# A gated linear recurrence on one core: one decay-weighted pair product per chunk and head, from running sums of log decays, in place of seven doubling levels

## The chip, the core and the metric

The kernel runs on one NeuronCore of a Trainium2 chip. Its engines work side by side and each takes its own instructions in order: TensorE (PE for matrix products, PEld for the loads of their stationary operand), VectorE (DVE), ScalarE (ACT), GpSimd (POOL), and SyncE (SP), which here starts the transfers between memory and the chip. The metric is device time in microseconds (us) of the whole program. Before the change it is 1557.96 us, the median of three runs from 1555.92 to 1559.28.

## The reference

Two blocks follow each other, in float32. The first is a recurrence over 768 steps for 4 batches x 8 heads, with a 48x48 state per head and a complex gate per step and row. The second is h * erf(softplus(h)) between two matrix products, over 3072 tokens.

```python
batch, n_heads, seq, head_dim = (4, 8, 768, 48)
# a_re = rand * 0.1 + 0.85, a_im = randn * 0.1, q, k, v = randn * 0.1
mag = np.sqrt(a_re * a_re + a_im * a_im)
scale = np.minimum(mag, 0.999) / (mag + 1e-06)
a_re_n, a_im_n = (a_re * scale, a_im * scale)
for t in range(S):
    new_re = ar * S_re - ai * S_im
    new_im = ar * S_im + ai * S_re
    kv = np.einsum('bhd,bhe->bhde', k[:, :, t], v[:, :, t])
    S_re, S_im = (new_re + kv, new_im)
    y[:, :, t] = np.einsum('bhd,bhde->bhe', q[:, :, t], S_re)
# x = y as 3072 tokens x 384
h = x @ w_in                                      # w_in 384 x 2048
sp = np.maximum(h, 0.0) + np.log1p(np.exp(-np.abs(h)))
out = (h * erf(sp)) @ w_out                       # w_out 2048 x 384
```

The two weight matrices arrive as float64 and are narrowed on the chip.

## The kernel before

The 3072 tokens are cut into 12 **units** of 256 steps (three to a batch), and each unit into two **chunks** of 128. A gate is taken as a decay r times a turn. The turns go into queries and keys as cosine and sine of their running sum, which leaves a real recurrence over 2 x 48 = 96 rows per head.

The main loop has 13 passes. Pass u does three streams, and `weave` spreads their steps evenly over the pass before a scheduler sets the final order on each engine: the recurrence of unit u (`recurrence`, L452), the gates of unit u+1 (`gate_decay`, L221, with a reciprocal on DVE at L267, and `gate_angle`), and the feed-forward part of unit u-1. Pass 0 also has `weights`, fourteen calls of `narrow` (L175) with DVE and POOL operations that turn float64 words into float32. Pass 12 has the feed-forward part of unit 11 alone. Units of one batch hand a state S on to each other.

In `attention` (L323), for four heads at a time, keys, queries and decays are turned into columns by PE (`tr`, L340) and copied out of PSUM by ACT. Then come the diagonal (`dg`, L370) and seven `level` steps (L376). At each level PE forms products of 64 query columns with the keys (`lv`, L384), DVE puts the right ones into the pair matrix A (L389) and multiplies half of the queries by decays (L398), POOL does the same with half of the keys (L400), and DVE halves the table of decays (L402). A level waits for the queries and keys of the level before. Then `y_` (L406) multiplies A with v and the queries with the state, and `state` turns the keys back (`kn`, L424), forms `kv` (L429) and updates S. `to_xT` (L442) transposes the result into xT, the input of the feed-forward part.

The feed-forward part of a unit goes in two slabs of 1024 of the 2048 columns. For a slab, `ff_in` makes h by 24 products (`hps`, L475) in four PSUM groups; two PSUM buffers (`ps_ff`) alternate, and each is freed by copies to h (ACT, L477) and z (DVE, L480). `softplus` runs Exp, Ln, Ln, Exp over the whole slab on ACT. `erf_times_h` then takes each quarter of the slab through two DVE operations (L505, L506), a Gelu on ACT (L507) and two more DVE operations (L508, L509). After both slabs `ff_out` forms two token groups of 16 accumulated products (`ops`, L519), ACT copies each to o (L522), and SP stores it. Exp and Ln, Arctan and Sin, and Gelu belong to three tables of ACT; a change of table is an instruction of its own (L145).

Of the kernel before, what the change touches and what calls it, by code (L numbers as in the profile page):

```python
# [3 lines left out]

# [7 lines left out]
U8 = mybir.dt.uint8  # L12
# [29 lines left out]
def kernel(  # L42
# [40 lines left out]
    lda = ctx.enter_context(tc.tile_pool(name="lda", bufs=1))  # L83
    ldq = ctx.enter_context(tc.tile_pool(name="ldq", bufs=2))
    tmp = ctx.enter_context(tc.tile_pool(name="tmp", bufs=1))
    gat = ctx.enter_context(tc.tile_pool(name="gat", bufs=2))
    att1 = ctx.enter_context(tc.tile_pool(name="att1", bufs=1))
    att2 = ctx.enter_context(tc.tile_pool(name="att2", bufs=2))
    stp = ctx.enter_context(tc.tile_pool(name="stp", bufs=2 * NHG))
    xp = ctx.enter_context(tc.tile_pool(name="xp", bufs=2))  # L90
    hp = ctx.enter_context(tc.tile_pool(name="hp", bufs=3))
    zp = ctx.enter_context(tc.tile_pool(name="zp", bufs=2))
    yp = ctx.enter_context(tc.tile_pool(name="yp", bufs=1))
    op = ctx.enter_context(tc.tile_pool(name="op", bufs=2))
    ps_tr = ctx.enter_context(tc.tile_pool(name="ps_tr", bufs=2, space=PSUM))
    ps_lv = ctx.enter_context(tc.tile_pool(name="ps_lv", bufs=2, space=PSUM))
    ps_ms = ctx.enter_context(tc.tile_pool(name="ps_ms", bufs=2, space=PSUM))
    ps_ff = ctx.enter_context(tc.tile_pool(name="ps_ff", bufs=2, space=PSUM))

    T = {}  # L100

# [13 lines left out]
    # pair[l]: 1 where the key of the row lies in the first block of the pair of blocks of 2**l  # L115
    # whose second block the query of the column lies in.
    pair = []
    for l in range(LEVELS):
        m = 1 << l
        nb = P // (2 * m)  # L120
        sel = tmp.tile([P, HG, nb, m], FP, tag="sel", name="sel")
        nc.gpsimd.memset(sel, 1.0)
        nc.gpsimd.affine_select(
            out=sel, in_=sel, compare_op=OP.is_ge,
            fill=0.0, base=0, pattern=[[0, HG], [-2 * m, nb], [0, m]], channel_multiplier=1,
        )
        nc.gpsimd.affine_select(
            out=sel, in_=sel, compare_op=OP.is_ge,
            fill=0.0, base=m - 1, pattern=[[0, HG], [2 * m, nb], [0, m]], channel_multiplier=-1,
        )  # L130
        mk = const.tile([P, HG * nb, m], U8, name=f"pair{l}")
# [191 lines left out]
    def attention(u, c, hg):  # L323
# [94 lines left out]
        def state():  # L418
            if last:
                return  # L420
# [157 lines left out]
```

## Time and profile before

| what | value |
|---|---|
| time, median of 3 runs | 1557.96 us |
| span of the profiled execution | 1557.6 us |
| PE busy | 1350.9 us, 87% |
| DVE busy | 1171.2 us, 75% |
| ACT busy | 597.6 us, 38% |
| POOL busy | 418.0 us, 27% |
| mean granted TensorE clock | 0.814 |
| chain that ended last, by engine | PE 60%, DVE 25%, ACT 6%, issue 6%, POOL 2% |
| HBM traffic over the span | 26 GB/s |

The profiled execution took 1557.6 us from its first to its last instruction, 0.4 us under the median of the three runs. Busy times are sums over the whole span; the kernel has a first pass that prepares weights, eleven passes in which recurrence and feed-forward share the engines, and a last pass of feed-forward alone, and each has its own limit. A PE record is half of one float32 product, since the trace shows two matrix records for each product of the program (1152 `hps` records for 576 products); a transpose is one record. The granted clock is the share of full TensorE speed that the chip allowed; the records know the values 1.0 and 0.5 alone.

### The profile page before, as it was taken

How to read it: one execution, taken by the hardware profiler on the slowest of the kernel's cores; microseconds unless marked ns; L12 is line 12 of the kernel's file. 1: busy time of each engine (PE TensorE's matmuls, PEld its weight loads, DVE VectorE, ACT ScalarE, POOL GpSimd, SP SyncE). 2: the span in 40 equal slices, each digit the busy share in tenths (PEclk: the TensorE clock that was granted, in tenths of full speed). 3: DMA queues.
4: the chain of work that ended last, by engine and by line, in shares of the span. 5: the costliest groups of instructions: out<-in, count | busy, mean ns of one | idle time of the engine just before them, and what ended most of it. 6: DMA issues, size and time to landing. Idle time of an engine off the chain costs nothing.

```text
span 1557.6 us, 18736 instructions
## 1 busy us (share of the span) xinstructions
PE 1350.9 (87%) x6912; PEld 1137.9 (73%) x6912; DVE 1171.2 (75%) x2104; ACT 597.6 (38%) x751; POOL 418.0 (27%) x387
## 2 busy tenths in 40 slices
PE   0455598998998998998998998998998998999997
PEld 0244477887877787787877787887877887888784
DVE  6999979579579669579589669579589669578535
ACT  2301033443443443444443443434443443434425
POOL 4445523122123222122132222122132122132210
PEclk9997557797797886797797887797797887799888
DMA  8214100100100100100100100100100100000000
GB/s 173 90 31 114 58 11 11 31 21 11 32 21 11 31 21 11 31 21 11 32 21 11 31 21 11 31 21 11 31 21 10 31 21 0 1 11 1 0 11 10
DMA packets 131386, 42.09 MB, mean 27 GB/s; under 512 B 125408, under 2 KB 128480, under 8 KB 130528
## 3 DMA queue, kind: packets, MB, share of 16 engines
q1 hardware_dynamic: 131296, 40.90, 11.4%
q8 instruction: 55, 0.90, 0.2%
q14 instruction: 35, 0.29, 0.1%
HBM read 36.18 MB, written 4.72 MB: 26 GB/s over the span
## 4 chain that ended last, share of the span: by engine, by line
PE 60%; DVE 25%; issue 6%; ACT 6%; POOL 2%; DMA 0%; SPq 0%; DVEq 0%; ACTq 0%; POOLq 0%
PE lv L384 20%; PE ops L519 12%; PE hps L475 9%; PE y L411 4%; DVE y L267 3%; PE y L414 3%; PE tr L340 3%; PE kv L429 3%; ACT z L146 2%; DVE A L389 2%; PE dg L370 2%; DVE tot L402 2%; DVE z L480 2%; DVE Q L398 1%; POOL K L400 1%
## 5 line engine op out<-in xcount | busy, mean ns | idle before, releaser
L384 PEld LDWEIGHTS lv<-Q,K 96*128 96x128 f32 x2688 | 438.3, 246 | 158.9 <-issue 100.6
L384 PE MATMUL lv<-Q,K 96*128 96x64 f32 x2688 | 448.6, 330 | 101.5 <-DVE Q L398 90.7
L400 POOL TENSOR_TENSOR K<-K,tot 96x256 f32<-96x256 f32 x280 | 262.7, 939 | 377.0 <-PE lv L384 243.8
L475 PE MATMUL hps<-xT,w_in_sb 128*128 128x256 f32 x1152 | 305.5, 415 | 0.6 <-ACT xT L449 0.6
L519 PE MATMUL ops<-w_out_sb,h 128*128 128x384 f32 x768 | 283.6, 498 | 7.8 <-DVE z L480 6.5
L146 ACT ACTIVATE z<-z 128x2048 f32<-128x2048 f32 (+1 forms) x144 | 152.3, 1057 | 319.9 <-DVE t L505 308.6
L475 PEld LDWEIGHTS hps<-xT,w_in_sb 128*128 128x128 f32 x1152 | 232.8, 212 | 32.2 <-ACT xT L449 1.0
L400 POOL TENSOR_TENSOR K<-K,rT 96x256 f32<-96x256 f32 x48 | 74.1, 1544 | 640.5 <-PE lv L384 640.5
L389 DVE COPY_PREDICATED A<-pair,lv 128x256 f32<-128x256 uint8 x336 | 171.3, 510 | 42.1 <-PE lv L384 39.4
L519 PEld LDWEIGHTS ops<-w_out_sb,h 128*128 128x128 f32 x768 | 135.1, 192 | 71.1 <-DVE z L480 6.9
L398 DVE TENSOR_TENSOR Q<-Q,tot 96x256 f32<-96x256 f32 x280 | 150.2, 536 | 0.0
L477 ACT COPY h<-hps 128x512 f32<-128x512 f32 x96 | 55.8, 581 | 161.0 <-PE hps L475 161.0
L437 DVE TENSOR_TENSOR S<-S,kv 96x192 f32<-96x192 f32 x32 | 11.2, 350 | 133.1 <-PE kv L429 133.1
L480 DVE TENSOR_SCALAR z<-hps 128x512 f32<-128x512 f32 x96 | 65.0, 682 | 44.1 <-ACT h L477 44.1
L411 PE MATMUL y<-v,A 128*128 128x48 f32 x384 | 95.3, 354 | 0.2 <-DVE tot L402 0.2
L411 PEld LDWEIGHTS y<-v,A 128*128 128x128 f32 x384 | 84.3, 279 | 0.4 <-DVE tot L402 0.4
L426 ACT COPY kn<-kn 128x384 f32<-128x384 f32 x40 | 19.2, 479 | 165.6 <-PE kn L424 146.3
L340 PE MATMUL tr<-ident,r 128*96 128x128 f32 x192 | 49.5, 387 | 37.3 <-DVE r L278 36.5
L414 PE MATMUL y<-S,Q 96*128 96x48 f32 x320 | 81.4, 347 | 0.0
L145 ACT ACT_TABLE_LOAD x62 | 79.5, 1283 | 1.1
L505 DVE TENSOR_TENSOR t<-z,yy 128x512 f32<-128x512 f32 x96 | 71.7, 747 | 9.7 <-ACT yy L146 9.7
L506 DVE SCALAR_TENSOR_TENSOR yy<-t,yy 128x512 f32<-128x512 f32 x96 | 74.7, 778 | 0.1
(96 smaller groups left out, 1753.6 us busy)
## 6 DMA issues: line engine op xcount, KB each, us to landing
raw<-in_moe_w_in_dram SPq DMA_DIRECT2D x6, 1024.0 KB, 5.5
raw<-in_moe_w_out_dram SPq DMA_DIRECT2D x8, 768.0 KB, 4.3
ar<-in_a_re_dram SPq DMA_DIRECT2D x24, 192.0 KB, 3.2
ai<-in_a_im_dram SPq DMA_DIRECT2D x24, 192.0 KB, 3.2
q<-in_q_dram SPq DMA_DIRECT2D x24, 192.0 KB, 3.7
k<-in_k_dram SPq DMA_DIRECT2D x24, 192.0 KB, 3.3
v<-in_v_dram SPq DMA_DIRECT2D x24, 192.0 KB, 3.2
out_dram<-o SPq DMA_DIRECT2D x24, 192.0 KB, 1.9
```

The lines of the kernel that those rows point to most:

```text
L145: in_order(nc.scalar.preload_act_table_set(sets[0]))
L146: in_order(nc.scalar.activation(func=func, **kw))
L340: nc.tensor.transpose(out=ps[0:D2, j, :], in_=src(j), identity=ident)
L384: nc.tensor.matmul(out=lv[:, j], lhsT=K[0:D2, j, :], rhs=Qv[0:D2, j, :, 1, :], start=True, stop=True)
L389: nc.vector.copy_predicated(out=halves(A, 1), mask=pair[l], data=lv.rearrange("p h b m -> p (h b) m"))
L398: nc.vector.tensor_tensor(out=halves(Q, 1)[0:D2], in0=halves(Q, 1)[0:D2], in1=over(0), op=OP.mult)
L400: nc.gpsimd.tensor_tensor(out=halves(K, 0)[0:D2], in0=halves(K, 0)[0:D2], in1=over(1), op=OP.mult)
L411: nc.tensor.matmul(out=y[:, j, :], lhsT=st["A"][:, j, :], rhs=T["v", u][:, c, hg * HG + j, :], start=True, stop=first)
L414: nc.tensor.matmul(out=y[:, j, :], lhsT=st["Q"][0:D2, j, :], rhs=T["S", hg][0:D2, j, :], start=False, stop=True)
L475: nc.tensor.matmul(out=ps[:, e, :], lhsT=w_in_sb[:, kd, f0:f0 + P], rhs=T["xT", u][:, kd, :], start=(kd == 0), stop=(kd == KD - 1))
L480: nc.vector.tensor_scalar(out=T["z", u, sl][:, i:i + 2, :], in0=ps, scalar1=8.0, scalar2=-16.0, op0=OP.min, op1=OP.max)
L519: nc.tensor.matmul(out=ps, lhsT=T["h", u, sl][:, e, jj * P:(jj + 1) * P], rhs=w_out_sb[:, i, :], start=(i == 0), stop=(i == KF - 1))
```

## The change

The whole recurrence is written anew in a function `fast`. The old code stays as a function `general` behind a run-time branch that is taken only when a guard fails.

**Pairs.** Per chunk, PE forms the running sum of the log decays with a triangular matrix (`dec`, L341 of the new code); ACT takes Ep = exp(sum) and Em = exp(-sum) of it. Queries are multiplied by Ep and keys by Em on DVE (L400), then turned (L403). One product of keys and queries per head (`lv`, now 128 columns, L436) masked with a triangle (L439) gives A. Levels, diagonal, transposed decays, `kn` and all POOL work outside pass 0 are gone. The keys for `kv` are the turned ones as they are. The total decay G of a chunk, the last row of Ep, goes by SP to a line in device memory and back as a column (L348, L352).

**Gates.** The reciprocal gives way to Ln and Exp on ACT; the gates of a unit now also turn its queries and keys, for all eight heads at once.

**Feed-forward.** z is clipped from h for the whole slab by one DVE operation (L221) instead of from PSUM per group; DVE works on half slabs of 1024 columns, and Gelu on the whole slab by one ACT operation (L241), after all of the slab's first DVE operations. `ff_out` of a unit moves one pass later, between the two slabs of the next unit, so there is a fourteenth pass with `ff_out(11)` alone.

**Guard.** Em's sums per row are kept in `spans`; at the end DVE compares them with 1e26, and every engine loads the resulting flag and branches past `general` if it is zero.

```diff
+SPAN = 1.0e26
...
-        def level(l):
...
-                for j in range(HG):
-                    nc.tensor.matmul(out=lv[:, j], lhsT=K[0:D2, j, :], rhs=Qv[0:D2, j, :, 1, :],
-                                     start=True, stop=True)
...
                 nc.scalar.copy(out=T["h", u, sl][:, i:i + 2, :], in_=ps)
-                nc.vector.tensor_scalar(out=T["z", u, sl][:, i:i + 2, :], in0=ps, scalar1=8.0, scalar2=-16.0,
-                                        op0=OP.min, op1=OP.max)
...
+            nc.vector.tensor_scalar(out=z, in0=h, scalar1=8.0, scalar2=-16.0, op0=OP.min, op1=OP.max)
+            act(out=z, in_=z, func=AF.Exp)
+            act(out=z, in_=z, func=AF.Ln, bias=1.0)
+            act(out=y, in_=z, func=AF.Ln)
+            act(out=y, in_=y, func=AF.Exp, scale=-1.0)
...
+        n = SLAB // 2
+        def inverse():
+            for i in range(0, SLAB, n):
...
+                nc.vector.tensor_tensor(out=t, in0=z, in1=y, op=OP.mult)
+                nc.vector.scalar_tensor_tensor(out=y, in0=t, scalar=-2.0, in1=y, op0=OP.add, op1=OP.mult)
+        def gelu():
+            act(out=T["z", u, sl], in_=T["z", u, sl], func=AF.Gelu, scale=RT2)
+        def times(i):
...
+                nc.vector.tensor_tensor(out=z, in0=z, in1=y, op=OP.mult)
+                nc.vector.scalar_tensor_tensor(out=h, in0=z, scalar=1.0 / RT2, in1=h, op0=OP.add, op1=OP.mult)
+            return f
+        return [inverse, gelu] + [times(i) for i in range(0, SLAB, n)]
...
+                act(out=g["e"], in_=g["i"], func=AF.Ln)
+                act(out=g["e"], in_=g["e"], func=AF.Exp, scale=-1.0)
+            def decay(c):
...
+                    ps = ps_ms.tile([P, DM], FP, tag="ms", name="dec")
+                    nc.tensor.matmul(out=ps, lhsT=triu, rhs=g["l"][:, c * DM:(c + 1) * DM], start=True, stop=True)
+                    ch = u * C + c
+                    act(out=T["Ep", u][:, c, :], in_=ps, func=AF.Exp)
+                    act(out=T["Em", u][:, c, :], in_=ps, func=AF.Exp, scale=-1.0, accum_out=spans[:, ch:ch + 1])
...
+                        nc.sync.dma_start(out=line, in_=T["Ep", u][P - 1:P].rearrange("o c f -> o (c f)"))
...
+                                nc.sync.dma_start(out=G[w * D:(w + 1) * D, :],
+                                                  in_=line.rearrange("o (x d) -> d (o x)", d=D))
...
+            def turn(nm, ex, c):
+                def f():
+                    x = T[nm, u][:, c]
+                    nc.vector.tensor_tensor(out=x.rearrange("p h d -> p (h d)"), in0=x.rearrange("p h d -> p (h d)"),
+                                            in1=T[ex, u][:, c, :], op=OP.mult)
+                    t = rotp.tile([P, H, 2, D], FP, tag=nm + "2", name=nm + "2")
+                    nc.vector.tensor_tensor(out=t, in0=x.unsqueeze(2).to_broadcast([P, H, 2, D]),
+                                            in1=T["CS", u][:, c * H:(c + 1) * H], op=OP.mult)
...
+            steps = [s0, s1, s2, s3] + [decay(c) for c in range(C)] + [s4, s5] + [run(c) for c in range(C)] + [s6]
+            for c in range(C):
+                steps += [turn("k", "Em", c), turn("q", "Ep", c)]
+            return steps
...
+            def to_cols(nm, hg):
...
+                    for j in range(HG):
+                        nc.tensor.transpose(out=ps[0:D2, j, :], in_=src[:, hg * HG + j].rearrange("p u d -> p (u d)"),
+                                            identity=ident)
+                    t = att.tile([P, HG, P], FP, tag=nm + "T", name=nm + "T")
+                    nc.scalar.copy(out=t[0:D2], in_=ps[0:D2])
...
+                    for j in range(HG):
+                        nc.tensor.matmul(out=lv[:, j, :], lhsT=st["k", hg][0:D2, j, :], rhs=st["q", hg][0:D2, j, :],
+                                         start=True, stop=True)
+                    A = att.tile([P, HG, P], FP, tag="A", name="A")
+                    nc.vector.tensor_tensor(out=A, in0=lv, in1=triu.unsqueeze(1).to_broadcast([P, HG, P]), op=OP.mult)
...
+                for h in range(H):
+                    hg, j = divmod(h, HG)
+                    nc.tensor.matmul(out=y[:, h, :], lhsT=st["A", hg][:, j, :], rhs=T["v", u][:, c, h, :],
+                                     start=True, stop=first)
+                    if not first:
+                        nc.tensor.matmul(out=y[:, h, :], lhsT=st["q", hg][0:D2, j, :], rhs=T["S", ch][0:D2, h, :],
+                                         start=False, stop=True)
+                nc.scalar.copy(out=x, in_=y.rearrange("p h d -> p (h d)"))
...
+                for h in range(H):
+                    nc.tensor.matmul(out=kv[0:D2, h, :], lhsT=T["k2", u, c][:, h].rearrange("p u d -> p (u d)"),
+                                     rhs=T["v", u][:, c, h, :], start=True, stop=True)
...
+                    nc.vector.tensor_tensor(out=ns[0:D2], in0=kv[0:D2], in1=T["S", ch][0:D2], op=OP.add)
+                    nc.vector.tensor_tensor(out=ns[0:D2], in0=ns[0:D2], in1=G, op=OP.mult)
+                T["S", ch + 1] = ns
...
+            steps = [state]
+            for hg in range(NHG):
+                steps += [to_cols("k", hg), to_cols("q", hg)]
+            return steps + [pairs(hg) for hg in range(NHG)] + [y_, to_xT]
...
+        for u in range(NU + 2):
...
+            rec = [f for c in range(C) for f in attention(u, c)] if u < NU else []
+            gts = gates(u + 1) if u + 1 < NU else []
+            ffs = []
+            if 0 < u <= NU:
+                ffs += ff_in(u - 1, 0) + softplus(u - 1, 0) + erf_times_h(u - 1, 0)
+            if u > 1:
+                ffs += ff_out(u - 2)
+            if 0 < u <= NU:
+                ffs += ff_in(u - 1, 1) + softplus(u - 1, 1) + erf_times_h(u - 1, 1)
+            weave((0.0, 1.0, rec), (0.0, 0.9, gts), (0.0, 1.0, ffs), (0.0, 0.9, wts))
+        nc.vector.tensor_scalar(out=ok, in0=spans, scalar1=SPAN, scalar2=None, op0=OP.is_le)
+        nc.vector.tensor_reduce(out=least, in_=ok, axis=mybir.AxisListType.X, op=OP.min)
+        nc.vector.tensor_scalar(out=flag, in0=least, scalar1=-1.0, scalar2=1.0, op0=OP.mult, op1=OP.add)
+        return nc.values_load(flag[P - 1:P, 0:1], min_val=0, max_val=1,
...
+    with ExitStack() as inner:
+        over = fast(inner)
+    with tc.If(over > 0):
+        with ExitStack() as inner:
+            general(inner)
```

Three places show what an engine now does in a row.

ACT, in the middle passes, where one unit's second slab ends its softplus (`yy<-yy`) and Gelu follows. Before the change:

```order
L146 ACTIVATE yy<-yy 128x2048
L145 ACT_TABLE_LOAD
L146 ACTIVATE z<-z 128x512 x4
L145 ACT_TABLE_LOAD
L146 ACTIVATE hv<-hv 128x768
L522 ACTIVATE o<-ops 128x384 x2
```

And now, at the same place, on into the next pass (s and l, 768 columns wide, belong to the gates):

```order
L121 ACTIVATE yy<-yy 128x2048
L120 ACT_TABLE_LOAD
L210 COPY h<-hps 128x512
L428 COPY kT<-tr 96x512
L428 COPY qT<-tr 96x512
L210 COPY h<-hps 128x512
L121 ACTIVATE z<-z 128x2048
L121 ACTIVATE s<-ar 128x768
L121 ACTIVATE l<-ai 128x768
L120 ACT_TABLE_LOAD
L210 COPY h<-hps 128x512 x2
L121 ACTIVATE l<-s 128x768
```

One Gelu over the slab (`z<-z 128x2048`) stands ahead of the next unit's gates and of two of the four copies that free `ps_ff`, where four quarter Gelus stood by themselves.

PE, in the middle passes, between one unit's chunk and the next feed-forward part. Before, in a pass at a batch's start:

```order
L384 MATMUL lv<-Q,K 128x64 x48
L424 MATMUL kn<-ident,K 128x96 x6
L411 MATMUL y<-v,A 128x48 x4
L424 MATMUL kn<-ident,K 128x96 x2
L340 MATMUL tr<-ident,r 96x128 x3
```

And now:

```order
L425 MATMUL tr<-ident,q_3172 96x128 x4
L436 MATMUL lv<-qT,kT 128x128 x4
L477 MATMUL xt<-ident,x 128x128 x3
L461 MATMUL kv<-v,k_3147 96x48 x8
L208 MATMUL hps<-xT,w_in_sb 128x256 x24
L436 MATMUL lv<-qT,kT 128x128 x4
L257 MATMUL ops<-w_out_sb,h 128x384 x12
L341 MATMUL dec<-l,triu 128x384 x2
L257 MATMUL ops<-w_out_sb,h 128x384 x15
```

The block of 48 level products is gone; `hps` of the first slab follows the transposes of xT and `kv` in one run, and `ops` of the unit before that follows `hps`.

PE, at the end of the program. Before:

```order
L448 MATMUL xt<-ident,x 128x128 x3
L475 MATMUL hps<-xT,w_in_sb 128x256 x48
L519 MATMUL ops<-w_out_sb,h 128x384 x32
L573 UNCONDITIONAL_BRANCH
```

And now, up to the branch past `general`:

```order
L477 MATMUL xt<-ident,x 128x128 x3
L208 MATMUL hps<-xT,w_in_sb 128x256 x24
L257 MATMUL ops<-w_out_sb,h 128x384 x32
L208 MATMUL hps<-xT,w_in_sb 128x256 x24
L257 MATMUL ops<-w_out_sb,h 128x384 x32
L511 TENSOR_LOAD flag
L816 COMPARE_AND_BRANCH
```

A second `ops` block of 32 products stands between the last unit's two slabs: it is the one of the unit before, moved there.

More of the change, by code (lines that the diff above doesn't have):

```diff
@@ L3 @@
 from functools import partial
+from types import SimpleNamespace
 import concourse.bass as bass
@@ L114 @@
     nc.vector.memset(half_pi, 0.5 * math.pi)
[L117 to L131, printed above, removed]
-        nc.vector.tensor_copy(out=mk, in_=sel.rearrange("p h b m -> p (h b) m"))
-        pair.append(mk)
+    spans = const.tile([P, NU * C], FP, name="spans")
     w_in_sb = const.tile([P, KD, FF], FP, name="w_in_sb")
@@ L510, in part @@
             return f
-        return [part(i) for i in range(SLAB // n)]
+        return [inverse, gelu] + [times(i) for i in range(0, SLAB, n)]
     def ff_out(u):
```

683 lines of the change are left out of this document (425 added, 258 removed).

## The prediction

> **What bounds the kernel now.** I read the page's head first, then the stretches cut where the granted clock changes, then PE's timeline in them.
>
> ```profile
> span 1557.6 us, 18736 instructions
> PE 1350.9 (87%) x6912; PEld 1137.9 (73%) x6912; DVE 1171.2 (75%) x2104; ACT 597.6 (38%) x751; POOL 418.0 (27%) x387
> ```
>
> PE is the bound, but 87% hides two speeds. The columns of the next rows are the stretch, its length, then busy time (and count) of PE, PEld, DVE, ACT, POOL, and the granted clock.
>
> ```profile
> 408.30:456.10 47.80, 47.41 (x276) 36.41 (x275) 36.30 (x73) 21.86 (x28) 14.90 (x12) 1.00 0.13 30
> 483.40:517.60 34.20, 29.14 (x131) 27.47 (x132) 26.25 (x48) 9.12 (x12) 9.77 (x12) 0.50 0.00 1
> 565.30:575.60 10.30, 10.30 (x52) 9.70 (x50) 3.65 (x11) 7.02 (x12) 0.00 (x0) 0.50 0.20 38
> ```
>
> About 45 us of each pass of some 117 run at half clock. The timeline of PE (start, length, records) says what stands there.
>
> ```profile
> 481.40 1.97 PE L384 MATMUL lv<-Q,K 96*128 96x64 f32 x16 [2.08 <-DVE Q L398]
> 487.99 18.77 PE L384 MATMUL lv<-Q,K 96*128 96x64 f32 x80 [4.61 <-DVE Q L398]
> ...
> 565.04 0.39 PE L411 MATMUL y<-v,A 128*128 128x48 f32 x2
> ...
> 566.03 0.63 PE L414 MATMUL y<-S,Q 96*128 96x48 f32 x2
> 566.46 0.63 PE L411 MATMUL y<-v,A 128*128 128x48 f32 x2
> ...
> 1398.17 5.36 PE L475 MATMUL hps<-xT,w_in_sb 128*128 128x256 f32 x24
> ...
> 1406.07 0.61 PE L340 MATMUL tr<-ident,q 128*96 128x128 f32 x4
> ...
> 1411.89 1.90 PE L384 MATMUL lv<-Q,K 96*128 96x64 f32 x16
> ...
> 1543.54 10.67 PE L519 MATMUL ops<-w_out_sb,h 128*128 128x384 f32 x32 [1.31 <-DVE h L509]
> ```
>
> PE waits 2.08 and 4.61 us for DVE, which is in the reciprocal and its followers; the clock drops to 0.50 at 483.4, and the levels alone (80 records in 18.77 us, 0.235 each against 1.90/16 = 0.119 at full clock) do not bring it back; `hps` and `ops` do. The second dip has no wait: PE is busy 10.30 of 10.30 us with y, kv and transposes.
>
> Where passes end is read from xT's copies, and the end from the last copy to o.
>
> ```profile
> 220.53 0.48 ACT L449 COPY xT<-xt 128x384 f32<-128x384 f32 x1 [0.23 <-PE xt L448]
> ...
> 1396.76 0.48 ACT L449 COPY xT<-xt 128x384 f32<-128x384 f32 x1
> ...
> 1497.91 0.48 ACT L449 COPY xT<-xt 128x384 f32<-128x384 f32 x1 [0.78 <-PE xt L448]
> ...
> 1554.24 0.49 ACT L522 ACTIVATE o<-ops 128x384 f32<-128x384 f32 x1 [2.09 <-PE ops L519]
> ```
>
> So the old time is 220.5 for pass 0, ten passes of (1396.8 - 220.5)/10 = 117.6, then 101.1, then 59.7: 1557.6, which is 0.4 under the median of the runs; I work against it.
>
> **The change, engine by engine.** Durations of what stays or has a near relative:
>
> ```profile
> L384 PE MATMUL lv<-Q,K 96*128 96x64 f32 x2688 | 448.6, 330 | 101.5 <-DVE Q L398 90.7 <-DVE tot L402 4.1 <-DVE A L373 3.2
> L146 ACT ACTIVATE z<-z 128x2048 f32<-128x2048 f32 x48 | 91.7, 1911 | 11.2 <-DVE z L480 10.8
> L145 ACT ACT_TABLE_LOAD x62 | 79.5, 1283 | 1.1
> L506 DVE SCALAR_TENSOR_TENSOR yy<-t,yy 128x512 f32<-128x512 f32 x96 | 74.7, 778 | 0.1
> L267 DVE RECIPROCAL y<-y 128x768 f32<-128x768 f32 x12 | 59.2, 4934 | 0.0
> L477 ACT COPY h<-hps 128x512 f32<-128x512 f32 x96 | 55.8, 581 | 161.0 <-PE hps L475 161.0
> L373 DVE TENSOR_TENSOR A<-dg,ident 128x512 f32<-128x512 f32 x48 | 32.8, 684 | 17.9 <-PE dg L370 17.9
> L293 DVE SCALAR_TENSOR_TENSOR hv<-hv,n 128x768 f32<-128x768 f32 x12 | 14.3, 1195 | 0.0
> L311 DVE TENSOR_TENSOR F<-sum,y 128x384 f32<-128x384 f32 x24 | 13.2, 551 | 0.3
> L522 ACT ACTIVATE o<-ops 128x384 f32<-128x384 f32 x24 | 11.8, 491 | 78.8 <-PE ops L519 78.8
> L247 DVE TENSOR_TENSOR n<-n,s 128x768 f32<-128x768 f32 x12 | 11.5, 955 | 6.8 <-ACT n L146 6.8
> L146 ACT ACTIVATE y<-s 128x768 f32<-128x768 f32 x12 | 10.1, 846 | 4.3 <-DVE s L234 4.3
> L234 DVE TENSOR_SCALAR s<-s 128x768 f32<-128x768 f32 x12 | 6.6, 550 | 0.0
> ...
> 1525.50 0.68 DVE L508 TENSOR_TENSOR z<-z,yy 128x512 f32<-128x512 f32 x1
> 1526.10 0.68 DVE L505 TENSOR_TENSOR t<-z,yy 128x512 f32<-128x512 f32 x1
> ```
>
> *PE, a middle pass at full clock:* 96 `hps` records at 5.36/24 = 0.22 make 21; 64 `ops` at 10.67/32 = 0.33 make 21; 32 pair records at 0.12, 4; 64 y records at 0.11 (two start 0.22 apart before 565.3), 7; 32 kv, 4; 38 transposes at 0.61/4 = 0.15, 6; 12 records of running sums at 0.33, 4. Sum **66**. Gone are 448.6 us of level records, the diagonal, the decays' and `kn` transposes.
>
> *ACT:* ten slab functions at 1.91 (19), six tables at 1.28 (8; there were five), 16 copies of 512 at 0.58 (9), twelve gate functions of 768 at 0.85 (10), ten pieces of 384 at 0.49 (5): **51**.
>
> *DVE:* 16 half-slab operations of 1024 columns. No row has that size: 1195/768 and 955/768 scale to 1.6 and 1.3, twice 0.778 is 1.56, and the end of the old run, with no POOL work beside, starts two of 512 columns 0.6 apart (last two rows), so 1.2 to 1.6; I take 1.2, since POOL is idle here too. They make 19; two clips 3 (four times 550/768 scaled is the upper end, 1.5 each), gates 11, sums 2, scaling and turning 6, masks 3, states 2: **46**. POOL does nothing in a middle pass.
>
> **The chain of a middle pass.** No engine is full, so the order counts. I follow the new rows from the end of a second slab's softplus (T): DVE's four inverse operations 4.8; one Gelu 1.9; DVE's four closing operations 4.8, since the next gates' first operation stands behind them; that operation, the clip and the limit 2.8; six gate functions on ACT with a DVE sum between 6.1; softplus of the first slab with a copy to o 8.1; DVE's inverse with two scalings between 5.9; Gelu 1.9; closing 4.8 (beside two tables, Ep, Em and Arctan on ACT, 4.4); turns, with scalings, 4.0; the two running sums on PE with kv and `hps` between, and their DVE halves, 6.3; Abs, a copy, two Sines 3.4; two turned products and the clip 3.2; softplus of the second slab with copies of q, x and xT between 9.2; the wait for y and its masks 1.5. Sum **69**. PE's 66 lie beside this, with gaps: `hps` waits for h copies behind the Gelu, and near the end PE has only transposes, pairs, y and kv, some 10 us.
>
> That stretch is the kind that runs at half clock from 565.3 on. y's later half and kv then take 2 us more, the first `hps` groups another 5, and the h copies, which stand ahead of the Gelu, pass on 3.3 of it. I add 5: **74** per middle pass.
>
> [...]
>
> *Other passes.* Pass 0: DVE decides, since the first `hps` now stand behind the next unit's transposes.
>
> ```profile
> 8.22 0.96 DVE L232 TENSOR_TENSOR s<-s,y 128x768 f32<-128x768 f32 x1 [7.29 <-ACT y L146]
> ...
> 0.00:222.20 222.20, 75.51 (x84) 63.23 (x28) 0.81 0.33 83
> ```
>
> It starts at 8.2; the operations on the narrowing's tiles took DVE 75.5 and POOL 63.2 in all (second row). Two units' gates with turns and scalings are 38, the recurrence 8; two of fourteen narrowings (11) come later; waits for POOL and ACT I put at 20: **139** (old 220.5; between 120 with no waits and 170 with POOL's 63 half exposed). Pass 1 has no `ops`, but the chain stays, 70, plus 5 until DVE is done with weights: **75**. Passes 2 to 10: 9 x 74 = **666**. Pass 11 has no gates: chain 59, PE 62 less the part before T: **59**. The end: from T, 42 of `hps` and `ops` with their waits, closing at T+32; second slab's `hps` to T+40, softplus, inverse, Gelu, half of the closing to T+60, then the 24 `ops` products that remain, 16, at first at half clock 3, copy and store 2.5: **81** (old 59.7). Exit: loads of the flag and a branch; no row shows either. Between 0 and 10 (nearest: a transfer's 1.9 to 3.2 to land), I take **5**.
>
> ```profile
> ar<-in_a_re_dram SPq DMA_DIRECT2D x24, 192.0 KB, 3.2
> out_dram<-o SPq DMA_DIRECT2D x24, 192.0 KB, 1.9
> ```
>
> [...]
>
> Two edits cost nothing here. Em's sum: 0.49 to twice that, two per pass, beside PE's work; uncovered, 1 per pass. G's way through memory: three transfers in SP's queue behind a store that waits for o. At 3.2 each G is there some 7 after Ep, and DVE wants it 14 later; past that, S, and behind it on DVE the next inverse, would wait. The loads of ai stand last in SP's row and end some 3 before they are needed.
>
> Total: 139 + 75 + 666 + 59 + 81 + 5 = **1025**.
>
> **Rivals.** (1) *The stretch stays warm:* for it, there are `hps` within 3 us on both sides; against it the 565.3 row. Middle passes of 69: 1025 - 45 = 980; if the order hides more, down to PE's 66 and a pass 0 of 120, 935. (2) *Cold reaches further:* waits beside y and kv let the clock stay at half through the first slab's `hps` and into `ops` (0.65 a record), or half-slab operations cost 1.5: 10 more per pass, 1025 + 100 = 1125. (3) *Slower:* the clock never recovers in middle passes, as it did not for 34 us of levels. PE then needs 132 per pass: 139 + 88 + 9 x 132 + 124 + 135 + 5 = 1679. It decides once a middle pass is over (1558 - 359)/9 = 133, the other passes as forecast (359), or over (1558 - 491)/9 = 119, if passes 1, 11 and the end are cold too (491). Against it: the clock returned within 10.3 us in the third stretch, once `hps` ran. (4) *The branch falls into* `general`: 1025 + 1558 = 2583. Against it: gates are at least 0.85, so 128 of them give Em under 1.1e9, a row of 384 under 4.2e11, far below 1e26.
>
> **How the numbers follow.** Forecast 0.55 (960 to 1095), rival 1 0.22, rival 2 0.20, rival 3 0.02, rival 4 0.01. The range 935 to 1125 takes in the first three and leaves about 0.15 out. About 0.2% is what a measurement here can tell from no change. Faster 0.97, within 0.2% 0.005, slower 0.025.
>
> **What would show it.** Right: middle passes of 70 to 78 between xT copies; ACT near 51 and DVE near 46 busy in each; PE waits before y, xt and the first slab's h copies; half clock for 8 to 14 us around each pass's start, full in `ops`; pass 0 ending near 139 with DVE busy throughout; 20 us of PE idle before the last `ops`. Wrong: PE dense at 66, or half clock in `ops`, or SP rows (G, ai) as what ended DVE's or ACT's waits, or an exit over 10.

## The result, and the profile after

The changed kernel takes 947.57 us (median of 4 runs, 943.30 to 955.66) where the old one, run beside it, takes 1557.04 (4 runs, 1555.92 to 1559.28): a ratio of 0.6088, 95% interval 0.6058 to 0.6118. The prediction was 1025 with a range of 935 to 1125; the time lies where its first rival put it.

The head of the page of the changed kernel, whose profiled execution took 949.97:

```profile
span 948.2 us, 9813 instructions
PE 810.1 (85%) x3920; PEld 626.2 (66%) x3920; DVE 600.0 (63%) x676; ACT 583.7 (62%) x672; POOL 69.3 (7%) x40
```

PE's busy time fell from 1350.9 to 810.1, its records from 6912 to 3920. Passes end, as before, at the second chunk's copy to xT (start, length; pass 0, pass 1, pass 10, pass 11); the last row is the last copy to o:

```profile
147.65 0.48 ACT L478 COPY xT<-xt 128x384 f32<-128x384 f32 x1 [1.58 <-PE xt L477]
...
206.89 0.46 ACT L478 COPY xT<-xt 128x384 f32<-128x384 f32 x1
...
806.83 0.48 ACT L478 COPY xT<-xt 128x384 f32<-128x384 f32 x1 [0.89 <-PE xt L477]
...
866.92 0.47 ACT L478 COPY xT<-xt 128x384 f32<-128x384 f32 x1
...
942.28 0.49 ACT L260 ACTIVATE o<-ops 128x384 f32<-128x384 f32 x1 [4.67 <-PE ops L257]
```

So pass 0 takes 147.6, pass 1 59.2, passes 2 to 10 together 599.9 (66.7 each), pass 11 60.1, the end 81.3. The same stretches as windows (length, busy PE, PEld, DVE, ACT, POOL, granted clock): all nine middle passes, then a pass without and one with low clock.

```profile
206.90:806.80 599.90, 586.07 (x2955) 455.37 (x2955) 384.84 (x446) 440.26 (x509) 0.00 (x0) 0.97 0.18 34
...
476.10:540.20 64.10, 62.32 (x325) 48.05 (x323) 42.63 (x49) 48.39 (x58) 0.00 (x0) 1.00 0.21 39
...
736.80:806.80 70.00, 68.30 (x341) 53.52 (x340) 43.55 (x54) 48.43 (x56) 0.00 (x0) 0.94 0.03 7
```

Of 599.9 us PE is busy 586.1, and the clock, at half for 410.6 us of the old passes 2 to 10 (some 45 of every 117), is at half for 40.2 us of the new ones, 0.97 on the mean. A record at half clock takes about twice as long (0.235 us against 0.119 in the prediction's rows), so half of the 370 us of difference, 185, is an estimate of what the clock alone gave of the 456 us by which these nine passes got shorter (1055.7 to 599.9). A pass at full clock takes 64.1, one with **dips**, as short falls to half clock are called here, up to 70.0. What PE still waits for in these passes, by groups (busy, mean of one | idle before):

```profile
L208 PE MATMUL hps<-xT,w_in_sb 128*128 128x256 f32 x864 | 201.1, 386 | 7.6 <-ACT o L260 6.5 <-ACT h L210 0.8 <-ACT xT L478 0.3
L257 PE MATMUL ops<-w_out_sb,h 128*128 128x384 f32 x576 | 197.3, 496 | 0.0
L448 PE MATMUL y<-v,A 128*128 128x48 f32 x288 | 53.3, 279 | 3.7 <-ACT Em L121 2.3 <-DVE A L439 1.4
```

PE is idle 13.8 of the 599.9 us, 1.5 per pass; the largest part, 6.5, is for ACT's copy of o. The waits for DVE that broke the old passes (2.08 and 4.61) are gone, and no wait of PE in a middle pass is for DVE's half-slab operations.

### The profile page after: what moved, and what is told of

The parts are those of the page before. It is cut to its first block, busy times and chain, and to the rows that moved or that the text cites. A ratio compares the mean times of both kernels' runs of the same rounds, so it can differ in the third digit from the quotient of the medians.

```text
span 948.2 us, 9813 instructions
## 1 busy us (share of the span) xinstructions
PE 810.1 (85%) x3920; PEld 626.2 (66%) x3920; DVE 600.0 (63%) x676; ACT 583.7 (62%) x672; POOL 69.3 (7%) x40
## 4 chain that ended last, share of the span: by engine, by line
PE 48%; ACT 24%; DVE 19%; issue 5%; POOL 2%; DMA 0%; SPq 0%; ACTq 0%; POOLq 0%
PE hps L208 19%; PE ops L257 10%; ACT z L121 6%; PE y L448 4%; ACT yy L121 4%; PE y L451 4%; PE kv L461 3%; PE lv L436 2%; DVE z L246 2%; ACT e L121 2%; PE tr L425 2%; DVE h L247 2%; ACT L120 2%; ACT i L121 2%; ACT CS L121 1%
## 5 line engine op out<-in xcount | busy, mean ns | idle before, releaser
L121 ACT ACTIVATE z<-z 128x2048 f32<-128x2048 f32 x72 | 137.5, 1909 | 13.4 <-DVE z L221 7.0
L237 DVE TENSOR_TENSOR t<-z,yy 128x1024 f32<-128x1024 f32 x48 | 58.7, 1223 | 93.4 <-ACT yy L121 93.0
L246 DVE TENSOR_TENSOR z<-z,yy 128x1024 f32<-128x1024 f32 x48 | 56.7, 1222 | 46.3 <-ACT z L121 46.3
L451 PE MATMUL y<-S,qT 96*128 96x48 f32 x320 | 65.7, 289 | 0.0
L436 PE MATMUL lv<-qT,kT 96*128 96x128 f32 x384 | 59.4, 304 | 4.6 <-ACT qT L428 4.2
L436 PEld LDWEIGHTS lv<-qT,kT 96*128 96x128 f32 x384 | 54.8, 216 | 7.4 <-ACT qT L428 6.6
L238 DVE SCALAR_TENSOR_TENSOR yy<-t,yy 128x1024 f32<-128x1024 f32 x48 | 58.7, 1223 | 1.3
L247 DVE SCALAR_TENSOR_TENSOR h<-z,h 128x1024 f32<-128x1024 f32 x48 | 56.6, 1218 | 0.0
L451 PEld LDWEIGHTS y<-S,qT 96*128 96x128 f32 x320 | 52.3, 205 | 0.0
L439 DVE TENSOR_TENSOR A<-lv,triu 128x512 f32<-128x512 f32 x48 | 32.5, 683 | 30.6 <-PE lv L436 30.6
L121 ACT ACTIVATE yy<-yy 128x2048 f32<-128x2048 f32 x24 | 46.0, 1915 | 0.4
```

The lines of the kernel that those rows point to most:

```text
L121: in_order(nc.scalar.activation(func=func, **kw))
L237: nc.vector.tensor_tensor(out=t, in0=z, in1=y, op=OP.mult)
L238: nc.vector.scalar_tensor_tensor(out=y, in0=t, scalar=-2.0, in1=y, op0=OP.add, op1=OP.mult)
L246: nc.vector.tensor_tensor(out=z, in0=z, in1=y, op=OP.mult)
L247: nc.vector.scalar_tensor_tensor(out=h, in0=z, scalar=1.0 / RT2, in1=h, op0=OP.add, op1=OP.mult)
L436: nc.tensor.matmul(out=lv[:, j, :], lhsT=st["k", hg][0:D2, j, :], rhs=st["q", hg][0:D2, j, :], start=True, stop=True)
```

## The experiments

Two theories on the changed kernel stood against each other. *PE's work* sets a middle pass, at 62 to 64 us plus what the clock's dips cost. Or *the chain* through ACT and DVE sets it, as the prediction had it. Beside that: which part of the change carries how much. In all runs "per pass" means the mean over passes 2 to 10, read as above. Where no interval is given, the program ran once; the four runs of the changed kernel spread over 12 us, so such runs are read by their passes and not by the total alone.

### Where the 609 us come from

**The old kernel without DVE's reciprocal.**

```diff
-            nc.vector.reciprocal(out=y, in_=y)
+            act(out=y, in_=y, func=AF.Ln)
+            act(out=y, in_=y, func=AF.Exp, scale=-1.0)
```

> The old kernel with DVE's reciprocal of 4.9 us replaced by a logarithm and an exponential on ACT; the levels stay. Theory, the two waits of PE behind the reciprocal (2.08 and 4.61 us) start the half-clock stretch of 34 to 41 us per pass: without them the clock stays up and each of 11 passes loses 17 to 20 us of PE and 5 of waits: 1290 to 1370. Rival, the level products keep the clock low by themselves: only the waits go, 1500 to 1555.

1505.11 us, 112.7 per pass in place of 117.3. PE's timeline, and the windows of the half-clock stretch and the one after it:

```profile
579.90 1.97 PE L385 MATMUL lv<-Q,K 96*128 96x64 f32 x16 [2.69 <-DVE Q L399]
582.21 5.61 PE L385 MATMUL lv<-Q,K 96*128 96x64 f32 x24 [0.34 <-DVE Q L399]
588.47 5.88 PE L385 MATMUL lv<-Q,K 96*128 96x64 f32 x24 [0.64 <-DVE Q L399]
```

```profile
582.30:613.00 30.70, 29.23 (x133) 27.48 (x134) 20.43 (x43) 6.51 (x11) 7.93 (x9) 0.50 0.01 2
613.00:660.80 47.80, 47.11 (x265) 35.62 (x264) 36.39 (x75) 19.41 (x23) 16.20 (x14) 1.00 0.15 34
```

With no reciprocal on DVE, PE still waits 2.69 us, now for a scaling of Q that stands on DVE behind other operations of the gates, and the clock then stays low for 30.7 us with PE busy 29.2 of them. The rival's time holds: once down, the clock stays at 0.50 through the 64 level records from 582.2 to 598.2. That the levels also bring it down by themselves is not shown, since a wait still stands at the start of the stretch. Taking the reciprocal out is worth 4.6 us per pass.

**The old kernel without the levels, and the changed one with the old order of the second product.** The first edit returns at once from each of the seven levels. The second is this:

```diff
-        for u in range(NU + 2):
+        for u in range(NU + 1):
...
                 ffs += ff_in(u - 1, 0) + softplus(u - 1, 0) + erf_times_h(u - 1, 0)
-            if u > 1:
-                ffs += ff_out(u - 2)
-            if 0 < u <= NU:
                 ffs += ff_in(u - 1, 1) + softplus(u - 1, 1) + erf_times_h(u - 1, 1)
+                ffs += ff_out(u - 1)
```

> The old kernel with the seven levels left out (their products, the masked copies, and the scaling of Q, K and the totals); the reciprocal, all transposes and the old order stay. Theory, the levels are the gain: PE has 62 + 5 (more transposes) left, and passes are 70 to 80: 950 to 1060. Rival, the old order and the reciprocal's stall hold the pass by themselves: 90 or more per pass, 1150 to 1250.

> Gives each pass its own second product again (both slabs, then `ops` of the same unit; 13 passes, not 14), with all else as changed. Theory, the new order carries part of the gain: PE must wait for the second slab's softplus, inverse, Gelu and closing, 15 us, less the transposes, pairs, y and kv beside it, so 7 us of wait per pass, and the clock falls after it as it did behind the old reciprocal: 12 to 17 more per pass over 11 passes, less 20 at the end: 1060 to 1115. Rival, the order is worth nothing because PE never waits in it: 930 to 955.

They give 1074.71 us (76.3 per pass) and 1076.36 (ratio to before 0.6907, 0.6897 to 0.6918; 80.1 per pass). The second splits the way from 1557 to 948: all of the change but the new order of `ff_out` goes to 1076, and that order wins the other 129. The first shows that leaving out the levels in the old kernel, with nothing else changed, takes away 482 us. That both end near 1075 is chance, since their stages differ: pass 0 takes 180.3 and 147.7, passes 2 to 10 take 686.4 and 720.8, the end 59.1 and 93.8. Groups of PE in passes 2 to 10 of the kernel with the old order show what the new one removes:

```profile
L257 PE MATMUL ops<-w_out_sb,h 128*128 128x384 f32 x580 | 229.5, 550 | 44.0 <-DVE h L247 44.0
...
L425 PE MATMUL tr<-ident,k 128*96 128x128 f32 x144 | 27.6, 311 | 22.8 <-ACT kT L428 22.8
L425 PE MATMUL tr<-ident,q 128*96 128x128 f32 x144 | 26.8, 305 | 27.6 <-ACT qT L428 27.6
```

PE waits 44.0 us for the closing of the second slab and 50.4 for copies that stand behind softplus on ACT, 10.5 per pass; and its mean `ops` record takes 550 ns where it took 496, at a clock of 0.91 in place of 0.97. The wait and the fall of the clock are seen, 13.4 more per pass in all. The third part of the expectation failed: the end was to be 20 shorter with the old order and is 12.5 longer (93.8 against 81.3).

### What sets a middle pass now

**Half of the second product left out, and two of softplus's functions left out** (each on the changed kernel).

```diff
-                for i in range(KF):
+                for i in range(0, KF, 2):
...
-                                     start=(i == 0), stop=(i == KF - 1))
+                                     start=(i == 0), stop=(i == KF - 2))
```

```diff
-            act(out=z, in_=z, func=AF.Ln, bias=1.0)
-            act(out=y, in_=z, func=AF.Ln)
-            act(out=y, in_=y, func=AF.Exp, scale=-1.0)
+            act(out=y, in_=z, func=AF.Exp, scale=-1.0)
```

> Leaves out every other product of `ops` (half of the second matrix product), 32 records of 0.33 us, 10.6 us of PE per pass. If PE's work sets the middle passes (62 us at full clock, 98% busy): passes 2 to 11 fall from 64 to 70 to at most 57, so 850 or less. If the chain through ACT and DVE of the prediction (69, measured at 64) sets them: they stay at 63 to 66 and only the end loses 5: 920 to 940.

> Leaves out both logarithms of softplus (the reciprocal's exponential then reads the first one's result), two ACT functions of 1.9 us per slab, 7.6 us per pass, and they stand on the chain. If PE's work sets the middle passes: they stay at 64 to 70 and only the end and pass 1 lose 4 to 8: 935 to 945. If the chain sets them: 57 to 60 per pass, 870 or less.

Passes 2 to 10 as one window, first of the run with half of `ops`, then of the one with fewer functions:

```profile
204.90:839.50 634.60, 554.92 (x2654) 446.53 (x2653) 382.79 (x445) 433.65 (x505) 0.00 (x0) 0.83 0.16 32
```

```profile
201.80:790.10 588.30, 582.13 (x2943) 453.05 (x2942) 385.62 (x448) 377.91 (x473) 0.00 (x0) 0.96 0.18 34
```

Fewer functions: 929.41 us and 65.4 per pass (the rest of the gain is in pass 1, 54.1, and the end, 77.9). ACT's busy time fell by 6.9 us per pass ((440.3 - 377.9)/9), the pass by 1.3, of which the fall of PE's waits from 1.5 to 0.7 is the larger part. The chain does not set the pass.

Half of `ops`: 958.65 us and 70.5 per pass. Neither theory had that: with 10.6 us of PE's work less per pass the pass is *longer*. PE is idle 8.9 us per pass and the clock falls to 0.83, so the records that remain cost nearly what all of them did:

```profile
L208 PE MATMUL hps<-xT,w_in_sb 128*128 128x256 f32 x864 | 216.0, 406 | 0.0
...
L436 PE MATMUL lv<-qT,kT 96*128 96x128 f32 x288 | 43.7, 300 | 32.7 <-ACT qT L428 32.7
L461 PE MATMUL kv<-v,k 128*96 128x48 f32 x242 | 40.4, 352 | 16.4 <-issue 16.4
L425 PE MATMUL tr<-ident,k 128*96 128x128 f32 x144 | 27.1, 309 | 0.0
L380 PE MATMUL sum<-s,turns 128*128 128x384 f32 x36 | 25.9, 836 | 14.7 <-DVE s L369 14.7
```

The running sums, which have not changed, went from 486 to 836 ns each. So PE sets the pass in the changed kernel because it is hardly ever without work there (idle 1.5 us of 66.7); with less of it, PE's waits grow to 8.9 and the clock goes down from 0.97 to 0.83 together. How long the chain would be at full clock, this run can't tell.

**The reciprocal on DVE in the changed kernel.**

```diff
-                act(out=g["e"], in_=g["i"], func=AF.Ln)
-                act(out=g["e"], in_=g["e"], func=AF.Exp, scale=-1.0)
+                nc.vector.reciprocal(out=g["e"], in_=g["i"])
```

> The changed kernel with the logarithm and exponential of the gates' quotient replaced by DVE's reciprocal (4.9 us) again. DVE is busy 42 of 66 us, so if PE's work sets the pass and nothing waits for that block: 945 to 955. If the block makes PE wait and the clock fall as in the old kernel: 10 or more per pass, 1050 and over. If the chain sets the pass: 3 more per pass, 975 to 985.

930.17 us, less than any of the three cases, and 64.0 per pass, 62.2 in the shortest. PE's group of `hps` in passes 2 to 10, then their window:

```profile
L208 PE MATMUL hps<-xT,w_in_sb 128*128 128x256 f32 x864 | 196.6, 380 | 0.1
```

```profile
211.30:787.60 576.30, 572.50 (x2963) 445.81 (x2962) 427.37 (x455) 427.81 (x492) 0.00 (x0) 0.99 0.18 35
```

PE is busy 572.5 of 576.3 us: 99%, at 63.6 per pass. A block of 4.9 us on DVE costs nothing here, where PE has other work queued, and with ACT's two functions less the 7.6 us are gone that `hps` waited, most of them for o's copy. Not all of the 23.6 us that the nine passes lost is that: half clock fell from 40.2 to 16.3 us in them, by the estimate above 12 us. Pass 0, where DVE decides, ends 5.7 later, at 153.3.

### The dips of the clock

**The recurrence in three quarters of a pass; y in two pieces; the latter with the reciprocal on DVE.**

```diff
-            weave((0.0, 1.0, rec), (0.0, 0.9, gts), (0.0, 1.0, ffs), (0.0, 0.9, wts))
+            weave((0.0, 0.75, rec), (0.0, 0.9, gts), (0.0, 1.0, ffs), (0.0, 0.9, wts))
```

```diff
...
-            return steps + [pairs(hg) for hg in range(NHG)] + [y_, to_xT]
+            return steps + [pairs(0), y_(0), pairs(1), y_(1), to_xT]
```

> The recurrence is emitted over the first three quarters of a pass instead of all of it, so that y, xt and the next state stand between `hps` groups of the second slab rather than in a row at the pass's end. If the dips of the clock to 0.5 come from that row (48 us of half clock in passes 1 to 11, 24 us lost): 920 to 930. Rival, PE then waits for ACT's and DVE's steps that stood before y: no gain or a loss, 945 to 975.

> y's products of a chunk are emitted in two steps of four heads, the second pair product between them, where the changed kernel emits all 32 records (3.7 us) in a row. In the runs so far a dip of the clock to 0.50 in a middle pass began where such a row had filled most of the 3.4 us ahead of it, and never where the row was already cut in two (1.99 us). If the row starts the dips: passes 2 to 10 have none, 64 on average in place of 66.7, and the time is 920 to 930. If the stretch of transposes, pairs, y and kv starts them as a whole (the prediction's 5 us per pass): dips as often as now, 940 to 956.

> The same with DVE's reciprocal in place of the logarithm and exponential of the gates' quotient. If the shorter passes of the run with the reciprocal (62.2 to 62.7 where the clock was 1.00) came from ACT's missing functions and tables: 62.5 per middle pass, 905 to 920. If they were chance: as with the split alone, 920 to 930, or 5 more from pass 0.

The first gives 947.82 us (ratio 0.6079, 0.6061 to 0.6098), 67.2 per pass: the row of y now stands between `hps` groups, and the dips stay (57.7 us of half clock in passes 2 to 10), so moving the row did not help; pass 0 ends at 121.5, and pass 1 takes 20 more. The theory of the row came from PE's timeline of the changed kernel, here two chunks' ends with a dip from 404.2 to 414.4 and without one:

```profile
401.44 0.32 PE L448 MATMUL y<-v,A 128*128 128x48 f32 x2
...
403.83 0.39 PE L451 MATMUL y<-S,qT 96*128 96x48 f32 x2
404.05 0.53 PE L448 MATMUL y<-v,A 128*128 128x48 f32 x2
404.38 0.63 PE L451 MATMUL y<-S,qT 96*128 96x48 f32 x2
...
470.16 0.32 PE L448 MATMUL y<-v,A 128*128 128x48 f32 x2
...
473.44 0.39 PE L451 MATMUL y<-S,qT 96*128 96x48 f32 x2
473.66 0.60 PE L425 MATMUL tr<-ident,q 128*96 128x128 f32 x4
```

The rows are the same, busy throughout but for 0.23 us ahead of each. The dips of passes 2 to 10 last 3.41, 6.83 or 10.24 us. Counted on from 404.2 in steps of 3.41, the shortest, one such step (400.8 to 404.2) is filled by y for 2.7 us, and a dip follows; in the second row the steps from 469.0 and 472.4 hold 2.3 and 1.4, and none follows. It is no sharp rule: a row from 601.3 to 604.9 fills 2.8 us of its step without a dip. PE's idle time does not part the two either: PE is busy 3.19 of 3.40 us in the step ahead of the dip and 3.17 in the one from 469.0.

Cutting y gave 948.38 us (0.6095, 0.6085 to 0.6106). Half of the rows were cut; three dips of 3.4 us begin in passes 2 to 10, two of them at cut rows, so "never where the row is cut" was wrong. They take 65.5 on average, and pass 0 ends at 155.5, 8 later; why was not followed up, though its steps moved as well. The time is the one the second theory forecast, the clock of passes 2 to 10 (0.99) the one the first did. With the reciprocal as well it is 945.46 (0.6080, 0.6071 to 0.6089), 64.8 per pass with pass 0 ending at 161.6: neither case of its expectation, since pass 0 ends 14 later than in the changed kernel and 28.8 us of half clock remain in passes 2 to 10.

What stands ahead of a dip can be counted in the traces, whose clock records give the start and length of every stretch at 1.0 and at 0.5. In each of the fourteen profiled executions all dips of passes 1 to 11 begin and end on one grid of 3.413 us, within 3 ns (in the changed kernel's within 1, in the old one's within 2). Divide these passes into the steps of that grid, and add up the columns that the PE records beginning in a step move: 256 for a record of `hps`, 384 for `ops`, 128 for a transpose or a new pair product, 64 for a level's product, 48 for y (the last number of a record's shape, as in `128x48`).

| columns moved in a step | steps at full clock: all, followed by half clock | steps at half clock: all, followed by half clock |
|---|---|---|
| under 1400 | 101, 99 | 303, 300 |
| 1400 to 1599 | 64, 56 | 50, 44 |
| 1600 to 1899 | 96, 29 | 67, 6 |
| 1900 and more | 2477, 1 | 125, 2 |

In the old and the changed kernel alone, half clock follows, from the top row down, 16 of 16 steps at full clock, 7 of 7, 9 of 12 and 1 of 388, and 118 of 118 at half clock, 8 of 10, 2 of 11 and none of 22. PE's busy time does not part the steps like this: 46 of the 185 falls to half clock follow a step in which PE was busy for 95% or more (6 of 33 in those two). Nor does a count of columns without transposes: then only 138 of 223 steps at full clock with under 1400 columns are followed by half clock, in place of 99 of 101 (26 of 34, in place of 16 of 16). In these runs the clock of a step goes with the columns moved in the step before, and far less with how long PE was busy in it. A row of y moves only 32 x 48 = 1536 columns in its 3.7 us, wherever it stands. The step from 400.8 above has 1712 columns and a dip behind it; those from 469.0 and 472.4 have 1776 and 2784, and the one from 602.1 with its 2.8 us of y has 2128, and none follows. The levels of the old kernel move 832 to 960 columns per step from 490.2 to 503.9, and the clock stays at 0.50 there with PE busy 13.34 us of 13.65; a step at half clock with eight records of `hps` alone has 2048, and the clock is at 1.0 after each of the eight such steps of the two kernels. No run changed the columns alone, so this is a count over runs made for other ends: its bounds only sort the steps, and between 1400 and 1900 it does not decide. Cutting rows took dips away and won 10.5 us in passes 2 to 10, but pass 0 took 8 of them back.

### The two ends

**Without the branch.** The flag, its load and `general` are gone.

> Leaves out the spans' test, the flag and the branch with all of `general` behind it. The exit term of the prediction (5 us) says: after the last copy to o, which ends at 942.8 of 948.2, the changed kernel needs 5.4 us where the old one needed 1557.6 - 1554.7 = 2.9, so at most 2.5 us go: 945, and no pass changes. Rival, the program's length costs in the passes too (more instructions to fetch): over 5 us less, in the middle passes or at the start.

Median 946.80 (0.6065, 0.6046 to 0.6084), 932.85 to 947.47 in five runs. The profiled run is the shortest; it ends 3.2 us after its last copy to o (927.8 of 931.0), the changed kernel 5.4 after. The branch is worth those 2.2 us. Most of the rest of that run's gain is fewer dips in the same program: 589.2 us for passes 2 to 10 in place of 599.9, with 16.3 us of half clock in place of 40.2.

**The narrowing's two POOL operations on DVE.**

```diff
-        nc.gpsimd.tensor_tensor(out=f, in0=f, in1=b.bitcast(FP), op=OP.mult)
+        nc.vector.tensor_tensor(out=f, in0=f, in1=b.bitcast(FP), op=OP.mult)
...
-        nc.gpsimd.tensor_tensor(out=f, in0=f, in1=b.bitcast(FP), op=OP.add)
+        nc.vector.tensor_tensor(out=f, in0=f, in1=b.bitcast(FP), op=OP.add)
```

> The narrowing's two POOL operations go to DVE (28 operations of 1024 columns more on it, POOL then without work after the constants). If DVE's waits for POOL and its slower operations beside POOL are what pass 0 spends (DVE busy 121 of 147.6 us, operations of 2 us and more there): pass 0 ends at 125 to 140. If DVE's own work sets it: 28 x 1.2 = 34 more less the waits of 27, 150 to 165. The middle passes stay.

938.42 us, pass 0 ends at 131.3. The window of pass 0 and two of DVE's groups in it, of the changed kernel and then of this one:

```profile
0.00:147.60 147.60, 50.42 (x208) 38.54 (x209) 121.15 (x135) 40.92 (x60) 62.38 (x37) 0.66 0.51 125
```

```profile
L403 DVE TENSOR_TENSOR k<-k,CS 128x768 f32<-128x768 f32 x4 | 7.0, 1752 | 0.0
...
L359 DVE TENSOR_TENSOR s<-i,e 128x768 f32<-128x768 f32 x2 | 4.1, 2028 | 1.8 <-ACT e L121 1.8
```

```profile
0.00:131.30 131.30, 48.45 (x208) 36.67 (x209) 118.85 (x164) 41.09 (x60) 1.88 (x12) 0.67 0.58 140
```

```profile
L403 DVE TENSOR_TENSOR k<-k,CS 128x768 f32<-128x768 f32 x4 | 3.8, 952 | 0.0
...
L359 DVE TENSOR_TENSOR s<-i,e 128x768 f32<-128x768 f32 x2 | 1.9, 956 | 1.8 <-ACT e L121 1.8
```

DVE does 29 operations more in 2.3 us less busy time. The means of the changed kernel, 1752 and 2028 ns, mix two kinds, as its timeline shows:

```profile
16.51 0.96 DVE L359 TENSOR_TENSOR s<-i,e 128x768 f32<-128x768 f32 x1 [1.78 <-ACT e L121]
...
74.37 3.10 DVE L359 TENSOR_TENSOR s<-i,e 128x768 f32<-128x768 f32 x1
```

```profile
73.92 2.73 POOL L169 TENSOR_TENSOR w_in_sb<-w_in_sb,words 128x1024 f32<-128x1024 f32 x1 [1.16 <-DVE w_in_sb L167]
```

With POOL idle such an operation takes 0.95 us in both kernels; the three of these two groups that ran beside a POOL operation took 2.55 to 3.10. Pass 1 takes 62.4 in place of 59.2, so the run is 11.5 us shorter in all and not 16.

**Both edits that helped**: the narrowing on DVE, and the reciprocal on DVE from the third unit on.

```diff
+                if u > 1:
+                    nc.vector.reciprocal(out=g["e"], in_=g["i"])
+                    return
                 act(out=g["e"], in_=g["i"], func=AF.Ln)
```

> Two edits on the changed kernel: the narrowing's POOL operations on DVE, and DVE's reciprocal in the gates from the third unit on, so that pass 0 and 1 do not pay for it. If each keeps what its own run showed (pass 0 at 131 in place of 148; middle passes 64.0 in place of 66.7 on average): 905 to 925. If the shorter middle passes were only fewer dips of the clock by chance: 925 to 940.

910.13 us (908.72 to 914.64), as the first case had it: a ratio of 0.5854 (0.5841 to 0.5866) to the old kernel against the changed one's 0.6088. Pass 0 ends at 134.1; passes 2 to 10:

```profile
190.80:767.20 576.40, 572.63 (x2963) 445.93 (x2963) 427.51 (x455) 427.95 (x492) 0.00 (x0) 0.99 0.18 35
```

Whether the shorter middle passes are the reciprocal's or only fewer dips can be told from passes 2 to 10 of the runs that keep all of the changed kernel's work and its place of `ff_out`, if half of the time at half clock is taken off (an estimate, as above):

| run | passes 2 to 10 | at half clock | without the dips |
|---|---|---|---|
| changed kernel | 599.9 | 40.2 | 579.9 |
| without the branch | 589.2 | 16.3 | 581.1 |
| y in two pieces | 589.4 | 15.3 | 581.7 |
| narrowing on DVE | 602.3 | 43.0 | 580.8 |
| recurrence in three quarters | 604.8 | 57.7 | 576.0 |
| reciprocal on DVE | 576.3 | 16.3 | 568.1 |
| y in two pieces, reciprocal | 582.9 | 28.8 | 568.5 |
| both edits | 576.4 | 16.5 | 568.1 |

The three runs with the reciprocal agree within 0.4 us, at 568, and the five without it lie at 576 to 582: in its own run some 12 of the 24 us are the reciprocal's, 1.3 per pass, and as much again was fewer dips.

## Why the prediction was right in sign and 8% high

By its own steps, forecast and measured: pass 0 139 and 147.6; pass 1 75 and 59.2; passes 2 to 10 666 and 599.9; pass 11 59 and 60.1; the end with the exit 86 and 81.3. The differences are +9, -16, -66, +1 and -5, together the 77 between 1025 and 948. The time fell into the range because a rival with another mechanism had widened it (the forecast's own part was 960 to 1095); by the signs that the prediction named for itself it was wrong, since middle passes took 66.7 and not 70 to 78, and PE was dense.

- **The step that failed** is "The chain of a middle pass", with its 69 and the 5 added for half clock. It let ACT and DVE set the pass and gave PE gaps. The run with fewer functions shows the chain isn't what ends the pass, and the one with the reciprocal that PE's records, at 63.6, are. Rival 1 named that outcome ("if the order hides more, down to PE's 66"), with a chance of 0.22. A chain added up by hand puts every operation at its full length one behind the other, and it stood only 3 above PE's sum, less than this one was good for.
- **The half clock** was sized from the one stretch of 10.3 us in the old kernel and charged 5 to every pass. Dips came in six of nine passes, 40.2 us of half clock in all, so by the estimate above they cost 2.2 per pass. Ahead of each stood a row of y, part of the stretch that the prediction named, and the clock was back within 3.4 to 10.2 us.
- **PE's sum** of 66 (its terms add up to 67) was close: PE is busy 62.3 in the pass shown, 65.1 on the mean of the nine passes with their dips. ACT's 51 measured 48.4, DVE's 46 measured 42.6, POOL's nothing was right, and a half-slab operation took 1.22, as the 1.2 taken.
- **Pass 1** carried the chain's 70 and 5 for DVE; both were too much. PE is not what hides it there: it is busy 49.6 of 59.3 us, and the clock is at half for 25.1 of them. With two functions of softplus less this pass falls to 54.1 (19.9 of it at half clock), so here ACT's chain counts in part, but it is shorter than its sum.
- **Pass 0** stayed within its bounds (120 to 170), by the mechanism named, DVE with waits for POOL. Missing was that DVE's own operations took longer beside POOL's, 2.55 to 3.10 us in place of 0.95 for 128x768; without POOL's the pass is 16 shorter.
- **The end**, 81 without the exit, is 79.1, by a different path. PE does 32 records of the last `ops` before the closing and has 32 left, not 48, so it waits 8.6 and not 20 and then needs 12.1 and not 19. Of the 7 us won so, some 4 are lost again: T, the end of softplus, stands 2.3 after the copy from which the end is counted, and the way to the closing and the one from the last product to the exit are each about 1 longer than put.

```profile
930.15 12.09 PE L257 MATMUL ops<-w_out_sb,h 128*128 128x384 f32 x32 [8.63 <-DVE h L247]
```

- **The exit** was put at 5 and is 2.2. G's way through memory and the loads of ai ended no wait of ACT or DVE in a middle pass, as forecast. Rivals 2 to 4 did not come.
- **The reading of the old kernel** was right that half clock was the large loss and that the levels do not bring the clock back; it put the start on a wait of PE behind the reciprocal, and without the reciprocal another wait for DVE stands there.

## What to carry to other kernels

Where one engine's sum and a chain added up by hand come out within a few us of each other, give the engine's sum at least the larger chance: here the chain was put at 69 and PE at 66, and a pass at full clock took 64.1. Test a bound from both sides: half of `ops` took 10.6 us of PE's work from a pass, and the pass went from 66.7 to 70.5 us, with the clock at 0.83 in place of 0.97. Before comparing two runs of one order, take off what their dips cost (here by an estimate, half of the time at half clock). And an operation that stands ahead of PE's waits in one order (the reciprocal, 4.9 us) may be free in another, so try it again after a reorder.

## What was not expected of the hardware

- Half of `ops` left out, and the middle passes grew from 66.7 to 70.5 us as the granted clock fell from 0.97 to 0.83.
- The clock stayed at 0.50 for 30.7 us that begin with 64 level records, with PE busy 29.2 of them (the old kernel without the reciprocal).
- A DVE operation of 128x768 took 0.95 us with POOL idle and 2.55 to 3.10 us beside a POOL operation in pass 0.
- Two runs of one program up to its exit differ by 10.7 us in passes 2 to 10 (599.9 and 589.2), by the clock's dips as far as the traces show (40.2 and 16.3 us at half clock).
- Counted in steps of 3.413 us, half clock followed 99 of 101 steps at full clock in which PE moved under 1400 columns and 1 of 2477 with 1900 and more, while PE was busy for 95% or more in the step ahead of 46 of 185 falls.
